# Router logits turned to token rows: transposes and an add on VectorE in place of an fp32 product

## The chip, the cores and the metric

The kernel runs on one core of one Trainium2 chip, as one launch. The metric is device time in microseconds (us). Before the change three runs took 1732.22 us in the median (1730.69 to 1737.27).

## The reference

A gated linear recurrence per head gives the token rows, and a mixture of eight experts works on them. The router weighs every expert for every token, with eight rounds of row and column normalisation (Sinkhorn) over all tokens:

```python
def _moe_ref(x, w_gate, w1, w2):          # x: 3072 tokens x 384, 8 experts, hidden size 1024
    logits = x @ w_gate
    logits = logits - logits.max()
    P = np.exp(logits)
    for _ in range(8):
        P /= P.sum(1, keepdims=True) + 1e-09
        P /= P.sum(0, keepdims=True) + 1e-09
        P *= N / E
    for e in range(E):
        h = np.maximum(x @ w1[e], 0.0)
        out += P[:, e:e + 1] * (h @ w2[e])
```

`x` is the recurrence's output: 4 sequences, 768 steps, 8 heads of 48.

## The kernel before

The work has two phases. Phase 1 runs the recurrence, and beside it the first two experts (0 and 1); phase 2 runs the other six. The change is in phase 1.

**Blocks.** The 3072 tokens are cut into 12 blocks of 256 (`SUB`), each of two chunks of 128. For block i VectorE and ScalarE prepare the gates and run a scan over them (`elem`, `chain`, `scan`): line 517 to 525 normalise (`x`, `y`, `z`), `cmul` (lines 429 to 434) is the scan's complex product, lines 535 to 546 build scaled keys (`kh`) and queries (`z` times `q`). DMAs lay keys and queries out by head (`ks` on SyncE's queue, `qs` on GpSimd's, line 569). Then `mix(i)` on TensorE transposes keys (`ktp`, line 590), makes scores (`sp`, 607), state updates (`U`, 600) and outputs (`y`, 624); VectorE masks the scores (610), carries the state (665 to 676), and splits the output into a high part `xh` and a rest `xl` (681).

**Experts.** While block i+1 is prepared and mixed, TensorE multiplies block i with experts 0 and 1 in 16 steps: `ph` (line 252, nine matmuls of 256 columns), ScalarE's `hh` and `hf` (275, 276), VectorE's rest `hl` (277), and, three steps later, `po` (213 to 215).

**Logits.** `logits(i)` is a generator that is advanced twice, after steps 1 and 3 of block i. The gate's weights are held as 16 columns, 8 high parts and 8 rests (`wgs`). Six matmuls make `lp`, 16 x 256: rows 0 to 7 from the high parts, rows 8 to 15 from the rests. ScalarE copies it to `ls`. Four steps of work later the logits are turned to token rows, 128 tokens x 8 per chunk, and put into `P`, which the Sinkhorn rounds use at the end of phase 1. `lp` and `lt` use the tag `s` of the pool `psS`, which has two buffers, as the key transposes and the scores do from block 1 on. So the buffers go round in the order in which TensorE's program asks for them: `lp`, `lt`, `ktp`, `sp`, and so on; what asks for `lt`'s buffer next is the scores.

**Order.** TensorE's order in phase 1 is written out by hand (`manual_schedule`). VectorE, ScalarE and SyncE are ordered in phase 1 by a scheduler from its own estimate of times, except for blocks 0 to 2, where lists of dependences fix part of it. Each engine works strictly along its order: what stands behind a waiting instruction waits too.

Of the kernel before, what the change touches and what calls it, by code (L numbers as in the profile page):

```python
# [6 lines left out]
F32 = mybir.dt.float32  # L7
F32R = mybir.dt.float32r
U8 = mybir.dt.uint8
AF = mybir.ActivationFunctionType  # L10
ALU = mybir.AluOpType
AX = mybir.AxisListType
# [4 lines left out]
E, F = 8, 1024  # L17
NF = F // 128
CH = 128
SUB = 256  # L20
# [56 lines left out]
class Net:  # L77
# [9 lines left out]
    def build(self):  # L87
        tc, nc = self.tc, self.nc
        DR = bass.MemoryType.DRAM
        PS = bass.MemoryType.PSUM  # L90
        with ExitStack() as ctx:
            dram = ctx.enter_context(tc.tile_pool(name="dram", bufs=1, space=DR))
            cst = ctx.enter_context(tc.tile_pool(name="cst", bufs=1))
            self.wp = ctx.enter_context(tc.tile_pool(name="wp", bufs=RING))

            self.ones = cst.tile([128, 128], F32, name="ones")
            nc.vector.memset(self.ones, 1.0)
            warm = cst.tile([128, 1], F32, name="warm")
            nc.scalar.activation(warm, self.ones[:, 0:1], AF.Abs_reciprocal_sqrt)
            self.ident = cst.tile([128, 128], F32, name="ident")  # L100
            nc.sync.dma_start(self.ident, self.idn)
            self.nident = cst.tile([128, 128], F32R, name="nident")
            self.mask = cst.tile([128, 4, CH], U8, name="mask")
            tri = cst.tile([128, CH], F32, name="tri")
            nc.sync.dma_start(tri, self.msk)
            for j in range(4):
                nc.gpsimd.tensor_copy(self.mask[:, j, :], tri)
            self.bm05 = cst.tile([128, 1], F32, name="bm05")
            nc.vector.memset(self.bm05, -0.5)
            self.wgs = cst.tile([128, NCT, 2 * E], F32R, name="wgs")  # L110
            self.two = cst.tile([2 * E, E], F32, name="two")
            nc.vector.tensor_tensor(self.two, self.ident[:2 * E, :E], self.ident[:2 * E, E:2 * E], ALU.add)
            wgr = cst.tile([128, NCT, E], F32, name="wgr")
            nc.sync.dma_start(wgr, self.wg)
            self.wgr = wgr
            self.P = cst.tile([128, self.ntt, E], F32, name="P")

            ns = self.N // SUB
            self.fl = cst.tile([128, ns * (NCT * NCH + 2) + 2 * NHALF], F32, name="fl")
            self.ok = cst.tile([128, 9], F32, name="ok")  # L120
            self.oki = cst.tile([1, 1], mybir.dt.int32, name="oki")
            self.wt = {}
            self.x_d = [dram.tile([128, NS, 2, NCT, 2, CH], F32, name=f"x_d{u}") for u in range(self.N // UN)]
            self.ye_d = [[dram.tile([128, C], F32, name=f"ye_d{u}_{i}") for i in range(self.ntt)] for u in range(2)]
            self.wd = [dram.tile([128, 4, 2 * 6 * 128], F32, name=f"wd{t}") for t in range(NT)]
            self.xf = [dram.tile([len(FORMS), 128, 2, TH], F32, name=f"xf{u}") for u in range(self.N // UN)]
            self.od = [dram.tile([128, C], F32, name=f"od{k}") for k in range(2 * NS)]

            with ExitStack() as c2, tc.manual_schedule(engines={mybir.EngineType.PE}):
                with ExitStack() as c1:  # L130
                    with ExitStack() as ca:
                        self.phase1(c1, ca)
                    self.phase2a(c2)
                with tc.manual_schedule(engines={mybir.EngineType.DVE, mybir.EngineType.Activation, mybir.EngineType.SP}):
                    self.phase2b(c2)
            flag = nc.values_load(self.oki[0:1, 0:1], min_val=0, max_val=1)
            with tc.If(flag < 1):
                with ExitStack() as c3:
                    self.general(c3)
# [557 lines left out]
    def logits(self, i):  # L697
        nc = self.nc
        xh, xl = self.xs[i]
        lp = self.psS.tile([2 * E, SUB], F32, tag="s", name=f"lp{i}")  # L700
        terms = [(ct, x) for ct in range(NCT) for x in (xh, xl)]
        if i == self.N // SUB - 1:
            terms.sort(key=lambda t: t[1] is xl)
        for q, (ct, x) in enumerate(terms):
            nc.tensor.matmul(lp, self.wgs[:, ct, :], x[:, ct, :], start=q == 0, stop=q == len(terms) - 1)
        ls = self.xp.tile([2 * E, SUB], F32, tag="ls", name=f"ls{i}", bufs=1)
        nc.scalar.activation(ls, lp, AF.Copy)
        yield
        lt = self.psS.tile([128, SUB // 128, E], F32, tag="s", name=f"lt{i}")
        for k in range(SUB // 128):  # L710
            nc.tensor.matmul(lt[:, k, :], ls[:, k * 128:k * 128 + 128], self.two, start=True, stop=True)
        n = SUB // 128
        nc.scalar.activation(self.P[:, i * n:(i + 1) * n, :], lt, AF.Copy)
        yield

    def check(self, sp, lg):
# [760 lines left out]
```

## Time and profile before

| what | value |
|---|---|
| median of three runs | 1732.22 us |
| profiled execution: span, first to last instruction | 1730.8 us |
| TensorE busy | 1707.6 us, 99% |
| VectorE busy | 1264.9 us, 73% |
| ScalarE busy | 731.4 us, 42% |
| TensorE's granted clock, mean | 0.999 |
| phase 1 | until about 586 us |

The page gives the span of the profiled execution and no other time for it. It was taken by the hardware profiler in one execution; the timed runs are other executions. "PE" in the rows is TensorE, "PEld" its weight load, "DVE" VectorE, "ACT" ScalarE, "POOL" GpSimd, "SP" SyncE. An fp32 matmul appears as several rows where the hardware takes it in passes. The share of an engine is a mean over stages: it says nothing on a stage that has another limit.

### The profile page before, as it was taken

What the parts mean: (1) busy time and instruction counts of PE and PEld (TensorE: products, weight loads), DVE (VectorE), ACT (ScalarE), POOL (GpSimd) and SP (SyncE); (2) the same over time, 40 slices, a digit from 0 to 9 for tenths busy, and PEclk for the clock granted to TensorE, in tenths of its full rate; (3) what the DMA queues carried; (4) which work ended last, traced back from release to release, by engine and by line L of the source; (5) the groups of instructions that cost most, each with busy time, mean ns of one, the idle gap of its engine ahead of it and who ended that gap; (6) DMA issues with size and microseconds to landing.
All of it is one profiled execution on the core that took longest, in us unless ns stands there. A gap on an engine that the chain in (4) does not pass through costs nothing.

```text
span 1730.8 us, 31183 instructions
## 1 busy us (share of the span) xinstructions
PE 1707.6 (99%) x11808; PEld 1677.0 (97%) x11808; DVE 1264.9 (73%) x2651; ACT 731.4 (42%) x1649; POOL 195.2 (11%) x368
## 2 busy tenths in 40 slices
PE   7999999999999999999999999999999999999998
PEld 5899999999999999999999999999999999999998
DVE  7888999899887888777755566656566655565654
ACT  8544555454543545554533333333433333433231
POOL 4211012110111323333200000000000000000000
PEclk9999999999999999999999999999999999999999
DMA  7534344543458867576567566567666556656560
GB/s 229 138 107 148 110 124 126 153 104 107 121 141 270 310 275 288 212 295 245 219 228 274 205 233 230 208 219 256 224 215 240 200 183 238 236 193 241 188 227 35
DMA packets 160829, 346.01 MB, mean 200 GB/s; under 512 B 15264, under 2 KB 101536, under 8 KB 160672
## 3 DMA queue, kind: packets, MB, share of 16 engines
q1 hardware_dynamic: 155264, 334.03, 55.5%
q0 software_dynamic: 4608, 9.52, 2.3%
q8 instruction: 95, 1.56, 0.4%
q14 instruction: 62, 0.51, 0.1%
q10 hardware_dynamic: 800, 0.39, 0.1%
HBM read 232.53 MB, written 98.70 MB: 191 GB/s over the span
## 4 chain that ended last, share of the span: by engine, by line
PE 91%; DVE 5%; DMA 2%; ACT 1%; issue 0%; SPq 0%; ACTq 0%; DVEq 0%
PE po L1089 12%; PE po L1090 12%; PE po L1088 12%; PE ph L252 10%; PE X L1144 4%; PE X L1145 4%; PE X L1146 4%; PE po L213 4%; PE po L214 3%; PE po L215 3%; PE Y L1144 3%; PE Y L1145 3%; PE Y L1146 3%; PE sp L607 2%; PE y L624 2%; PE U L600 2%
## 5 line engine op out<-in xcount | busy, mean ns | idle before, releaser
L1090 PE MATMUL po<-wd,hl 128*128 128x384 f32 x768 | 257.0, 335 | 0.0
L1089 PE MATMUL po<-wd,hh 128*128 128x384 f32 x768 | 256.6, 334 | 0.0
L1088 PE MATMUL po<-wd,hh 128*128 128x384 f32 x768 | 256.5, 334 | 0.0
L252 PE MATMUL ph<-xh,w 128*128 128x256 f32 x1152 | 225.9, 281 | 0.9 <-ACT xh L680 0.6
L252 PEld LDWEIGHTS ph<-xh,w 128*128 128x128 f32 x1152 | 185.4, 189 | 1.6 <-ACT xh L680 0.9
L252 PE MATMUL ph<-xl,w 128*128 128x256 f32 x576 | 154.5, 282 | 0.3 <-DVE xl L681 0.3
L1090 PEld LDWEIGHTS po<-wd,hl 128*128 128x128 f32 x768 | 144.2, 188 | 0.8 <-DVE hl L1166 0.2
L1088 PEld LDWEIGHTS po<-wd,hh 128*128 128x128 f32 x768 | 144.2, 188 | 0.0
L1089 PEld LDWEIGHTS po<-wd,hh 128*128 128x128 f32 x768 | 144.2, 188 | 0.0
L275 ACT ACTIVATE hh<-ph 128x256 fp32r<-128x256 f32 x160 | 61.3, 383 | 194.0 <-PE ph L252 193.4
L213 PE MATMUL po<-w,hh 128*128 128x384 f32 x384 | 138.6, 361 | 0.0
L215 PE MATMUL po<-w,hl 128*128 128x384 f32 x384 | 129.2, 336 | 0.6 <-DVE hl L277 0.6
L214 PE MATMUL po<-w,hh 128*128 128x384 f32 x384 | 129.0, 336 | 0.0
L1090 PE MATMUL po<-wc,hl 128*128 128x384 f32 x384 | 128.3, 334 | 0.0
L1089 PE MATMUL po<-wc,hh 128*128 128x384 f32 x384 | 128.3, 334 | 0.0
L1088 PE MATMUL po<-wc,hh 128*128 128x384 f32 x384 | 128.3, 334 | 0.0
L569 POOL DMA_DIRECT2D qs<-z x144 | 75.9, 535 | 424.2 <-DVE z L546 155.0
L252 PEld LDWEIGHTS ph<-xl,w 128*128 128x128 f32 x576 | 105.8, 189 | 0.5 <-DVE xl L681 0.5
L1165 ACT ACTIVATE hh<-X 128x384 fp32r<-128x384 f32 x64 | 31.5, 492 | 176.1 <-PE X L1146 176.1
L1071 DVE SCALAR_TENSOR_TENSOR oa<-po,P,oa 128x384 f32<-128x384 f32 x120 | 73.0, 614 | 20.6 <-PE po L1090 20.5
L277 DVE TENSOR_TENSOR hl<-hf,hh 128x256 fp32r<-128x256 f32 x160 | 68.6, 430 | 11.4 <-ACT hf L276 9.6
L213 PEld LDWEIGHTS po<-w,hh 128*128 128x128 f32 x384 | 72.6, 189 | 4.0 <-issue 3.4
(1826 smaller groups left out, 4396.1 us busy)
## 6 DMA issues: line engine op xcount, KB each, us to landing
wd<-wd SPq DMA_DIRECT2D x58, 768.0 KB, 5.8
wa<-wd SPq DMA_DIRECT2D x42, 768.0 KB, 4.3
wb<-wd SPq DMA_DIRECT2D x42, 768.0 KB, 5.6
wc<-wd SPq DMA_DIRECT2D x42, 768.0 KB, 4.5
xP<-xf SPq DMA_DIRECT2D x60, 384.0 KB, 4.3
raw<-in_w_dram SPq DMA_DIRECT2D x12, 1152.0 KB, 8.9
wd<-wc SPq DMA_DIRECT2D x16, 768.0 KB, 4.2
wd<-wa SPq DMA_DIRECT2D x16, 768.0 KB, 4.2
```

The costliest lines, as they stand in the source:

```text
L213: nc.tensor.matmul(po[k], hh[:, s], w2h, start=f == 0, stop=False)
L214: nc.tensor.matmul(po[k], hh[:, s], w2l, start=False, stop=False)
L215: nc.tensor.matmul(po[k], hl[:, s], w2h, start=False, stop=f == NF - 1)
L252: nc.tensor.matmul(ph, w[:, k, ct * 128:ct * 128 + 128], x[:, ct, :], start=q == 0, stop=q == len(terms) - 1)
L569: dma = eng.dma_start(dst[q:q + D - 2:NCT, :, :w], src[:, a, ct * NCH + c, :w])
L1071: V.scalar_tensor_tensor(oa[u, k], p, self.P[:, tt, e:e + 1], oa[u, k], ALU.mult, ALU.add)
L1088: nc.tensor.matmul(po[k], hh[:, s], w2[0], start=c == 1, stop=False)
L1089: nc.tensor.matmul(po[k], hh[:, s], w2[1], start=False, stop=False)
L1090: nc.tensor.matmul(po[k], hl[:, s], w2[0], start=False, stop=c == NF)
L1144: nc.tensor.matmul(ps, w[:, 0, k], x[:, 0], start=start, stop=False, skip_group_check=True)
L1145: nc.tensor.matmul(ps, w[:, 0, k], x[:, 1], start=False, stop=False, skip_group_check=True)
L1146: nc.tensor.matmul(ps, w[:, 1, k], x[:, 0], start=False, stop=True, skip_group_check=True)
```

## The change

The constant `two` (two 8 x 8 identities on top of each other) goes. Today one fp32 product per chunk, `ls` (16 x 128) as the stationary operand and `two` (16 x 8) as the moving one, turns the 16 rows to token rows and adds high part and rest; ScalarE copies the 128 x 2 x 8 result into `P`. Now a plain transpose per chunk, with a 16 x 16 identity, turns them to 128 x 16, and one VectorE reduction per block adds the halves from PSUM into `P`.

```diff
-            self.two = cst.tile([2 * E, E], F32, name="two")
-            nc.vector.tensor_tensor(self.two, self.ident[:2 * E, :E], self.ident[:2 * E, E:2 * E], ALU.add)
...
-        lt = self.psS.tile([128, SUB // 128, E], F32, tag="s", name=f"lt{i}")
-        for k in range(SUB // 128):
-            nc.tensor.matmul(lt[:, k, :], ls[:, k * 128:k * 128 + 128], self.two, start=True, stop=True)
         n = SUB // 128
-        nc.scalar.activation(self.P[:, i * n:(i + 1) * n, :], lt, AF.Copy)
+        lt = self.psS.tile([128, n, 2 * E], F32, tag="s", name=f"lt{i}")
+        for k in range(n):
+            nc.tensor.transpose(lt[:, k, :], ls[:, k * 128:k * 128 + 128], self.ident[:2 * E, :2 * E])
+        nc.vector.tensor_reduce(self.P[:, i * n:(i + 1) * n, :], lt.rearrange("p k (m e) -> p k e m", e=E), AX.X, ALU.add)
```

TensorE's order stays the same but for the two instructions of each block. The scheduler gives VectorE, ScalarE and SyncE another order in phase 1: VectorE's differs at many places, mostly by a residual `hl` that moves a few rows against a step of the recurrence. Line numbers of the changed kernel are 2 lower from line 112 on (711 is then the reduction).

On VectorE, block 0: the recurrence of block 1 is under way (`cm_a`, `cm_b` and `z` are the scan's products). Before:

```order
L432 TENSOR_TENSOR cm_a<-z_770 128x6x21 x2
L432 TENSOR_TENSOR cm_b<-z_770 128x6x21 x2
L433 TENSOR_TENSOR z_770<-cm_a,cm_b 128x6x7x3
L434 TENSOR_TENSOR z_770<-cm_a,cm_b 128x6x7x3
L432 TENSOR_TENSOR cm_a<-z_770 128x6x62 x2
```

The same place on VectorE now, with `lt` the transposed logits of block 0:

```order
L430 TENSOR_TENSOR cm_a<-z_768 128x6x21 x2
L430 TENSOR_TENSOR cm_b<-z_768 128x6x21 x2
L431 TENSOR_TENSOR z_768<-cm_a,cm_b 128x6x7x3
L432 TENSOR_TENSOR z_768<-cm_a,cm_b 128x6x7x3
L711 TENSOR_REDUCE P<-lt_990 128x16
L430 TENSOR_TENSOR cm_a<-z_768 128x6x62 x2
```

The reduction stands between two steps of the recurrence, and nothing else moved here.

On VectorE, block 5: the end of the recurrence of block 6 (`kh`, and `z` with `qk`), the start of block 7's (`x`, `y`, `z` with `x`), and residuals `hl` of the experts (`hl_4_7` is the last step of block 4, `hl_5_0` to `hl_5_3` are the first steps of block 5). Before:

```order
L545 TENSOR_TENSOR kh_4188<-x_4186,z_4088 128x1536
L521 SCALAR_TENSOR_TENSOR y_4758<-x_4757,y_4758 128x768
L681 TENSOR_TENSOR xl_3771<-y_1_3950,xh_3770 128x3x128
L546 TENSOR_TENSOR z_4088<-z_4088,qk_4089 128x12x128
L523 TENSOR_SCALAR x_4757<-y_4758 128x768
L277 TENSOR_TENSOR hl_4_7_4083<-hf_4_7_4084,hh_4_7_4082 128x256
L524 SCALAR_TENSOR_TENSOR x_4757<-zz_4759,x_4757 128x768
L277 TENSOR_TENSOR hl_5_0_4223<-hf_5_0_4224,hh_5_0_4222 128x256
L525 TENSOR_TENSOR z_4750<-z_4750,x_4757 128x12x128
L277 TENSOR_TENSOR hl_5_1_4238<-hf_5_1_4239,hh_5_1_4237 128x256
```

The same place on VectorE now:

```order
L275 TENSOR_TENSOR hl_4_7_4081<-hf_4_7_4082,hh_4_7_4080 128x256
L543 TENSOR_TENSOR kh_4186<-x_4184,z_4086 128x1536
L519 SCALAR_TENSOR_TENSOR y_4756<-x_4755,y_4756 128x768
L275 TENSOR_TENSOR hl_5_0_4221<-hf_5_0_4222,hh_5_0_4220 128x256
L544 TENSOR_TENSOR z_4086<-z_4086,qk_4087 128x12x128
L275 TENSOR_TENSOR hl_5_1_4236<-hf_5_1_4237,hh_5_1_4235 128x256
L521 TENSOR_SCALAR x_4755<-y_4756 128x768
L275 TENSOR_TENSOR hl_5_2_4273<-hf_5_2_4274,hh_5_2_4272 128x256
L522 SCALAR_TENSOR_TENSOR x_4755<-zz_4757,x_4755 128x768
L711 TENSOR_REDUCE P<-lt_4302 128x16
L523 TENSOR_TENSOR z_4748<-z_4748,x_4755 128x12x128
```

The residuals moved ahead of the steps of the recurrence: `hl_5_0` now stands before block 6's `z` with `qk`, and `hl_5_2` and the reduction before block 7's first `z`.

On VectorE, block 6: the scan of block 8. Before:

```order
L277 TENSOR_TENSOR hl_6_3_4961<-hf_6_3_4962,hh_6_3_4960 128x256
L429 TENSOR_TENSOR cm_a<-z_5430 128x12x32
L429 TENSOR_TENSOR cm_b<-z_5430 128x12x32
L433 TENSOR_TENSOR z_5430<-cm_a,cm_b 128x6x32
L434 TENSOR_TENSOR z_5430<-cm_a,cm_b 128x6x32
```

The same place on VectorE now:

```order
L427 TENSOR_TENSOR cm_a<-z_5428 128x12x32
L275 TENSOR_TENSOR hl_6_2_4935<-hf_6_2_4936,hh_6_2_4934 128x256
L427 TENSOR_TENSOR cm_b<-z_5428 128x12x32
L711 TENSOR_REDUCE P<-lt_4964 128x16
L431 TENSOR_TENSOR z_5428<-cm_a,cm_b 128x6x32
L432 TENSOR_TENSOR z_5428<-cm_a,cm_b 128x6x32
L275 TENSOR_TENSOR hl_6_3_4959<-hf_6_3_4960,hh_6_3_4958 128x256
```

The reduction stands behind `cm_b` of the last scan product of 32 columns, and the buffer of `lt`, which ScalarE's copy used to give back, is given back here.

## Rows read from the trace of the kernel before

**Rows 1.** The page's busy line: us, share of the span, instructions.
```profile
PE 1707.6 (99%) x11808; PEld 1677.0 (97%) x11808; DVE 1264.9 (73%) x2651; ACT 731.4 (42%) x1649; POOL 195.2 (11%) x368
```

**Rows 2.** TensorE's waits: who for whom, us in total, times, longest.
```profile
PE ktp L590 <- DMA ks<-kh: 1.1, 1, 1.1
```

**Rows 3.** Windows: busy us of each engine in a stretch of blocks 4 and 5.
```profile
255.00:300.00 45.00, 45.00 (x433) 44.14 (x431) 43.67 (x98) 22.15 (x55) 7.12 (x14) 1.00 0.46 125
```

**Rows 4.** The tile lt: duration ns min/median/max, first and last start.
```profile
L711 PE MATMUL lt<-two,ls x48: 251/251/272, 64.2 to 586.3; 16*128 16x8 f32 x48
L713 ACT ACTIVATE P<-lt x12: 182/190/191, 64.9 to 586.6; 128x16 f32<-128x16 f32 x12
```

**Rows 5.** Line 590, the key transposes, in the same columns.
```profile
L590 PE MATMUL ktp<-ident,ks x160: 257/259/316, 42.9 to 550.9; 112*128 112x112 f32 x160
```

**Rows 6.** Timeline of TensorE at block 5's logits: start us, us, what.
```profile
304.63 0.28 PE L252 MATMUL ph<-xh,w 128*128 128x256 f32 x1
304.84 0.61 PE L711 MATMUL lt<-two,ls 16*128 16x8 f32 x4
305.37 0.44 PE L213 MATMUL po<-w,hh 128*128 128x384 f32 x1
305.65 0.33 PE L214 MATMUL po<-w,hh 128*128 128x384 f32 x1
305.82 0.34 PE L215 MATMUL po<-w,hl 128*128 128x384 f32 x1
```

**Rows 7.** Timeline of TensorE at key transposes of block 6, then of block 3.
```profile
307.49 0.28 PE L252 MATMUL ph<-xh,w 128*128 128x256 f32 x1
307.61 0.55 PE L590 MATMUL ktp<-ident,ks 112*128 112x112 f32 x4
307.99 1.07 PE L607 MATMUL sp<-qs,ks 112*128 112x128 f32 x8
...
191.94 0.99 PE L590 MATMUL ktp<-ident,ks 112*128 112x112 f32 x8
192.70 0.42 PE L213 MATMUL po<-w,hh 128*128 128x384 f32 x1
192.95 0.33 PE L214 MATMUL po<-w,hh 128*128 128x384 f32 x1
```

**Rows 8.** Timeline of VectorE: two reductions.
```profile
580.37 0.17 DVE L725 TENSOR_REDUCE ok<-chk 128x1 f32<-128x12 f32 x1
588.90 0.27 DVE L744 TENSOR_REDUCE m<-mp 1x1 f32<-1x128 f32 x1
```

**Rows 9.** Timeline of VectorE and ScalarE at block 0's logits.
```profile
64.04 0.28 DVE L434 TENSOR_TENSOR z<-cm_a,cm_b 128x126 f32<-128x126 f32 x1
64.24 1.00 DVE L432 TENSOR_TENSOR cm_a<-z 128x372 f32<-128x372 f32 x2
64.85 0.19 ACT L713 ACTIVATE P<-lt 128x16 f32<-128x16 f32 x1
```

**Rows 10.** Timeline of VectorE and ScalarE at the first steps of block 5.
```profile
296.73 1.75 DVE L546 TENSOR_TENSOR z<-z,qk 128x1536 f32<-128x1536 f32 x1
298.91 0.38 ACT L276 ACTIVATE hf<-ph 128x256 f32<-128x256 f32 x1
300.40 1.75 DVE L525 TENSOR_TENSOR z<-z,x 128x1536 f32<-128x1536 f32 x1
```

**Rows 11.** Timeline of GpSimd at block 6's queries; DMA issues with median us to landing.
```profile
299.13 6.24 POOL L569 DMA_DIRECT2D qs<-z  x12 [33.48 <-ACT hh L275]
...
qs<-z POOLq DMA_DIRECT2D x144, 64.5 KB, 3.9
```

**Rows 12.** Timeline of VectorE and TensorE at block 6's logits and block 7's scores.
```profile
353.95 0.55 DVE L429 TENSOR_TENSOR cm_b<-z 128x384 f32<-128x384 f32 x1
...
355.50 0.73 PE L607 MATMUL sp<-qs,ks 112*128 112x128 f32 x5
```

**Rows 13.** VectorE's waits from 305 to 354.5 us.
```profile
DVE hl L277 <- ACT hf L276: 1.7, 3, 0.8
```

## The prediction, made before the changed kernel had run

> **What bounds the kernel now.** I read the busy line of the page first, then TensorE's waits, then the windows of single blocks, and only then the rows of the lines that change. The busy line [rows 1] puts TensorE at 99% of the span, VectorE at 73%, ScalarE at 42%. The reader should see that only TensorE's own time, or a new wait of TensorE, can move the end. TensorE's waits are few: behind the head, in which the weights come in, the longest single one is 1.1 us for the key tile of block 1 [rows 2], a DMA that VectorE's recurrence for that block feeds. The average share of VectorE hides its stages, so I read a stretch in which blocks 4 and 5 are worked on: in 45.00 us TensorE is busy 45.00 and VectorE 43.67 [rows 3]. There VectorE is 97% busy. It is not waited for, but it has little left to give, and the change puts work on it.
>
> **TensorE's part.** Today each block of 256 tokens issues two fp32 products; the trace has 48 passes for these 24, so two passes each, and 12 ScalarE copies of 0.19 us behind them [rows 4]. A transpose of fp32 data already stands in the kernel: 160 of them in the program (20 chunks of 8) and 160 passes in the trace [rows 5], one pass each. So a block goes from four passes to two. What a pass costs is read at block 5 [rows 6]: the four take 0.61 us and the last of them some 0.25, so they start (0.61 - 0.25) / 3 = 0.12 us apart. Two fewer are 0.24 us per block. Over 12 blocks that is 2.9 us.
>
> This has two ends. From the last matmul before the group (304.63) to the second after it (305.65) it is 1.02 us, where neighbours without the group would need 0.12 [rows 7] and 0.17 (305.65 to 305.82); so a group costs 0.73 today, and only half of that is passes. The rest is entry (0.21 instead of 0.12) and exit. Key transposes, which use 112 rows of the array, enter after 0.12, run 0.095 apart ((307.99 - 307.61) / 4) and are left after 0.25 more [rows 7]: two would fit into 0.12 + 0.19 + 0.25 = 0.56, a saving of 0.46 per block, 5.5 us in all. That is the good end. The bad end is nothing saved, if these narrow transposes take two passes each. I take 0.24, since the new transposes keep the 16-row operand of the products, the nearest row, and I see nothing in the change that touches entry and exit.
>
> The Trainium skill, "TensorEngine Tiling (Array Packing)", Key Properties, says that a change of tiling mode drains TensorE. If 16 rows count as another mode than 128, the drain stays with the transposes and the sum is 0.24 per block; if only the fp32 product caused it, it is 0.46. The late entry of the 16-row group against the 112-row one [rows 6, 7] agrees with the rule, but the trace has no 16-row transpose.
>
> **VectorE's part.** The sum of the two halves was free in the product; now a reduction of 32 values per partition, read from PSUM, does it. The trace has reductions of 12 values in 0.17 us and of 128 values from PSUM in 0.27 [rows 8]. I take 0.20; both ends stay in the range. Twelve of them are 2.4 us on VectorE, and ScalarE loses 12 x 0.19 = 2.3, which nobody was waiting for. The one small addition of two identities at the start goes too; VectorE was waiting for ScalarE before and after it, so it is worth nothing.
>
> What counts more than the 0.20 is where the reduction stands, since everything behind it on VectorE waits with it. Three places decide.
>
> Block 0. The reduction stands inside the recurrence of block 1, behind a step that ends at 64.04 + 0.28 = 64.32; the next recurrence step ran at 64.24 [rows 9]. The copy on ScalarE began at 64.85, when the products were done. With two passes fewer that is 64.6; the reduction ends at 64.8 and the recurrence goes on 0.55 us later than now. This is the chain that the 1.1 us wait hangs on, so that wait grows by 0.55, and block 0's own 0.24 is lost in it. TensorE's gain is then 11 x 0.24 = 2.6 us.
>
> Block 5. VectorE's order around it is another one: the last chain step of block 6 (z times q) now stands behind the residual of expert 0's first step of block 5, and the next chain, block 7's, behind the reduction. That residual can start when ScalarE's copy ends, 298.91 + 0.38 = 299.29, and takes 0.42; so the z step runs from about 299.75 and not from 296.73, 3.0 us later [rows 10]. Its 12 query DMAs go out over 6.24 us from 299.13 on and land 3.9 us after issue, so the sixth, with which the first chunk is complete, lands at 299.13 + 3.12 + 3.9 = 306.2, against scores that start at 307.99 [rows 7, 11]. A margin of 1.8 against 3.0: a wait of 1.2, of which I take 1.0, since both landing times are medians. The normalisation step of block 7 that ran at 300.40 cannot start before the reduction: the products end at 304.84 + 0.61 = 305.45, the transposes 0.24 earlier, the reduction at 305.4 at best. That is a chain some 5 us later [rows 6, 10].
>
> Block 6. The transposed logits sit in one of two PSUM buffers that the scores of the next block take over. ScalarE emptied it at once; now the scores wait for the reduction. It stands behind a step that runs from 353.95 to 354.50 in the old trace, and the scores start at 355.50 [rows 12]: without delay the reduction ends at 354.7 and nothing waits. But of block 7's 5 us, 1.0 is taken off by the wait above (TensorE slips too), and VectorE's idle time for hidden units, the part that can be made up, is 1.7 us between 305 and 354.5 [rows 13]. Some 2.0 us remain, so the reduction ends near 356.7 and TensorE waits 1.2. In the following blocks the same margin is used against a smaller lag; I put 0.2 us for them together.
>
> Waits: 0.55 + 1.0 + 1.2 + 0.2 = 2.95 us. With -2.6 that is +0.35 us on the profiled span of 1730.8. The page gives no other time for this execution; the span lies 1.4 us under the median of the timed runs, 1732.22, so I add the difference to the median: 1732.6 us.
>
> **Rivals.**
> - The gain is kept. VectorE catches up before anyone needs it and only block 0's 0.55 stays: 1732.2 - 2.6 + 0.55 = 1730.2. For it: later blocks are worked with far less VectorE pressure, and none of TensorE's waits in the trace is for a score mask. Against it: 43.67 of 45.00.
> - The transposes enter and leave like the key transposes: 11 x 0.46 = 5.1 saved, 0.55 lost, if nothing waits: 1727.7. For it: the same instruction in rows 7; against it: 16 rows.
> - The change doesn't do what it says: each narrow transpose takes two passes, nothing is saved and the waits stay: 1732.2 + 2.95 = 1735.2. Against it: rows 5.
> - Slower: VectorE's lag at block 5 isn't made up. The place is the PSUM buffer that the scores take over. If all 5 us arrive at block 6 and each of blocks 7 to 10 then pays 1.2 again, it is 0.55 + 1.0 + 5 + 4 x 1.2 = 11.4, less 2.6: 1741.0. It decides from the point where the chain falls behind more than 1 us per block (355.50 - 354.50). For it: 1.7 us of idle time against 5 of lag. Against it: once TensorE has waited, VectorE has that much more room.
>
> **How the numbers follow.** Chances: forecast 0.50, gain kept 0.22, quick transposes 0.08, two passes 0.08, slower 0.12. The forecast's own range is 1729 to 1737 (reductions of 0.17 to 0.27, waits of 0 to 6). The whole range of 1727 to 1739 takes in the first four and leaves the slow rival out. A change of 0.5% or 8.7 us is about what a measurement of this kernel can tell from no change. Faster by more than that needs 1723.5, beyond even the quick transposes with no wait: 0.02. Slower needs 1740.9, where the slow rival's middle is: 0.07 with a little for what I don't see. Within: 0.91.
>
> **What the profile of the changed kernel would show.** Right: 24 passes of the transposes instead of 48; some 0.8 us from the matmul before them to the second after them; 12 reductions near 0.20 us; TensorE's wait for the key tile of block 1 at 1.5 to 1.8 us; new waits of the scores for the reduction in block 6; ScalarE's 12 copies gone. The forecast is wrong if TensorE shows no new wait between 300 and 410 us, if the group takes 0.56 us, or if the scores of several blocks wait over 1 us each.

## The result and the profile after: 9.6 us slower

The changed kernel took 1741.82 us (median of five runs, 1741.45 to 1742.33) against 1732.22 (1730.69 to 1737.27): a ratio of 1.0053, with a 95% interval of 1.0042 to 1.0064. The profiled spans are 1740.6 and 1730.8 us, 9.8 apart. That is outside the predicted range of 1727 to 1739, and just over the 0.5% that the text called measurable.

The first two things to read in the new profile are the busy line of the page and the tile `lt`.

```profile
PE 1714.3 (98%) x11784; PEld 1681.9 (97%) x11784; DVE 1267.4 (73%) x2662; ACT 730.1 (42%) x1637; POOL 194.4 (11%) x368
```
```profile
L710 PE MATMUL lt<-ident,ls x24: 207/220/230, 64.2 to 589.8; 16*128 16x16 f32 x24
L711 DVE TENSOR_REDUCE P<-lt x12: 178/188/192, 64.5 to 590.2; 128x16 f32<-128x32 f32 x12
```

TensorE runs 24 instructions fewer than in [rows 1], yet is busy 6.7 us longer. The passes have halved against [rows 4], and the reduction costs 0.19 us. So what was changed did what it should. TensorE's timeline at block 5's logits, which answers to [rows 6], shows what it is worth.

```profile
304.38 0.28 PE L250 MATMUL ph<-xh,w 128*128 128x256 f32 x1
304.59 0.29 PE L710 MATMUL lt<-ident,ls 16*128 16x16 f32 x2
304.81 0.44 PE L211 MATMUL po<-w,hh 128*128 128x384 f32 x1
305.09 0.34 PE L212 MATMUL po<-w,hh 128*128 128x384 f32 x1
```

From the last matmul before the group to the second after it are 305.09 - 304.38 = 0.71 us instead of 1.02: 0.31 saved per block, 3.7 over twelve. The entry still takes 0.21 us, as before, and not 0.12.

To see where the time went I laid the two traces over one another, matmul by matmul (11,760 each, the logits' turning left out), and took each one's start in the new trace less its start in the old: the shift. A shift that grows is time lost. It goes in four stretches:

| stretch of the old trace | shift at its end | change |
|---|---|---|
| start to 306 us | -0.6 | -0.6 |
| 306 to 329 us | +5.0 | +5.5 |
| 329 to 630 us (start of phase 2) | +3.5 | -1.5 |
| 630 to 1724 us | +9.3 | +5.8 |

The last 0.5 us lie outside these matmuls, at the ends of the span. So there are two losses of nearly one size, in different phases, and they don't look alike.

**First loss: block 6's keys come late.** TensorE's waits from 295 to 340 us, and its timeline there, where [rows 7] had no gap:

```profile
PE ktp L588 <- DMA ks<-kh: 2.8, 1, 2.8
PE po L211 <- ACT yst L219: 0.6, 1, 0.6
```
```profile
306.91 0.28 PE L250 MATMUL ph<-xh,w 128*128 128x256 f32 x1
310.01 0.89 PE L588 MATMUL ktp<-ident,ks 112*128 112x112 f32 x4 [2.82 <-DMA ks<-kh]
310.69 1.94 PE L605 MATMUL sp<-qs,ks 112*128 112x128 f32 x8
312.28 0.67 PE L211 MATMUL po<-w,hh 128*128 128x384 f32 x1
312.75 0.52 PE L212 MATMUL po<-w,hh 128*128 128x384 f32 x1
```

The shift steps up by 3.0 us at 310.01. Behind the gap the matmuls are longer: 0.52 us for a row that takes 0.34 at 305.09. The windows of the same stretch show why (the number after the engines' busy times is the granted clock, as a share of full speed):

```profile
308.00:312.00 4.00, 1.99 (x11) 2.02 (x11) 3.90 (x10) 0.54 (x1) 1.26 (x3) 0.76 1.16 209
312.00:316.00 4.00, 4.00 (x29) 4.00 (x29) 3.17 (x13) 0.66 (x2) 0.00 (x0) 0.81 0.96 306
316.00:320.00 4.00, 4.00 (x44) 3.67 (x43) 3.79 (x19) 1.95 (x7) 0.00 (x0) 1.00 0.88 252
```

Means of 0.76 and 0.81 lie between the two levels, 1.2 and 2.4 GHz. After the idle 2.8 us a part of the work ran at the lower level; that is 1.7 of the 5.5 us (5.5 less the step of 3.0 and one of 0.8 at 334 us). From 316 on it is 1.00 again. So a wait of 2.8 us on the busiest engine cost some 4.7.

Why the keys are late is read backwards. SyncE's queue issues them from 300.11 on, 4.6 us later than before; 0.6 of that is the queue's own, which is busy with `xf<-x_d` until 300.02:

```profile
297.50 2.52 SPq L825 DMA_DIRECT2D xf<-x_d  x4
300.11 2.51 SPq L567 DMA_DIRECT2D ks<-kh  x4
302.72 1.01 SPq L220 DMA_DIRECT2D ye_d<-yst  x2
303.78 2.39 SPq L567 DMA_DIRECT2D ks<-kh  x2
```

The same queue in the kernel before:

```profile
295.50 1.87 SPq L569 DMA_DIRECT2D ks<-kh  x3
297.47 0.53 SPq L693 DMA_DIRECT2D x_d<-xl  x1
298.05 3.79 SPq L569 DMA_DIRECT2D ks<-kh  x6
```

The keys can be issued when VectorE has built `kh`, which starts 4.0 us later. Before, then now:

```profile
293.72 1.75 DVE L545 TENSOR_TENSOR kh<-x,z 128x1536 f32<-128x1536 f32 x1
...
297.70 1.75 DVE L543 TENSOR_TENSOR kh<-x,z 128x1536 f32<-128x1536 f32 x1
```

And `kh` is late because the recurrence of block 6 already was. VectorE's timeline, now:

```profile
278.62 0.42 DVE L275 TENSOR_TENSOR hl<-hf,hh 128x256 fp32r<-128x256 f32 x1
278.96 0.54 DVE L663 TENSOR_TENSOR tm<-st,U 112x384 f32<-112x384 f32 x1
...
279.82 0.55 DVE L670 TENSOR_TENSOR sa<-tm,rr 112x384 f32<-112x384 f32 x1
280.38 0.55 DVE L672 TENSOR_TENSOR sb<-tm,qs 48x384 f32<-48x384 f32 x1
280.95 0.55 DVE L673 TENSOR_TENSOR sb<-tm,rn 48x384 f32<-48x384 f32 x1
281.53 1.00 DVE L430 TENSOR_TENSOR cm_a<-z 128x372 f32<-128x372 f32 x2
```

And before:

```profile
277.90 0.28 DVE L434 TENSOR_TENSOR z<-cm_a,cm_b 128x126 f32<-128x126 f32 x1
278.10 0.99 DVE L432 TENSOR_TENSOR cm_a<-z 128x372 f32<-128x372 f32 x2
...
281.17 0.55 DVE L665 TENSOR_TENSOR tm<-st,U 112x384 f32<-112x384 f32 x1
...
283.07 0.55 DVE L672 TENSOR_TENSOR sa<-tm,rr 112x384 f32<-112x384 f32 x1
```

The state update (`tm`, `sa`, `sb`) used to stand among and behind these steps of the recurrence and now stands ahead of them: the step of 372 elements starts at 281.53 and not at 278.10. Its four rows make 2.2 us of these 3.4; the rest is a residual `hl` (0.3) and a delay from further ahead. So the rows that cost here are not residuals, which the section on the change names as most of what moved, and no reduction stands here. The delay lasts until `kh`. On the way VectorE even waits 1.9 us for ScalarE; in the kernel before it has no wait from 270 to 305 us:

```profile
292.21 0.96 DVE L515 SCALAR_TENSOR_TENSOR x<-sq 128x768 f32<-128x768 f32 x1 [1.87 <-ACT sq L510]
```

The chain to `kh` goes through ScalarE there (squares and roots), so the work that VectorE had done early doesn't bring the chain forward again. In a VectorE that is 97% busy [rows 3], the scheduler's other order is enough.

**Second loss: phase 2's second products run slower.** TensorE is busy 100 of 100 us there in both traces, the clock is 1.00, and the order is the same. The page's costliest group of the changed kernel, and the same instruction before (busy us, mean ns):

```profile
L1087 PE MATMUL po<-wd,hh 128*128 128x384 f32 x768 | 260.5, 339 | 0.0
```
```profile
L1089 PE MATMUL po<-wd,hh 128*128 128x384 f32 x768 | 256.6, 334 | 0.0
```

The pitch, the time from one start to the next (of those under 250 ns apart), tells more than the duration. For this product of `hh` and the weights' low part it went from 173.2 to 178.4 ns (768 of them), and for its twin with `wc` from 173.2 to 177.5 (384); for the product before it, of `hh` and the high part, from 173.7 to 174.7 (1152), and for the first products of the input forms (line 1142, which make the hidden units) from 173.9 to 172.6 (936). 0.768 x 5.2 + 0.384 x 4.3 + 1.152 x 1.0 - 0.936 x 1.3 = 5.6 of the drift's 5.8 us.

What differs there is not in the instructions. With the tile `two` went 32 bytes per partition of the SBUF pool in which the constants lie. Buffers are handed out from two ends of SBUF. Those after `two` from its end (in phase 2 the experts' weights, hidden units, copies and scratch) lie 32 bytes lower; those from the other end (input forms, staging, raw weights) stay. No row of the diff names these buffers, and no order of instructions shows that they moved.

### The profile page after: what moved, and what is told of

It reads as the page before. It is cut to its first block, busy times and chain, and to the rows that moved or that the text cites. A ratio compares the mean times of both kernels' runs of the same rounds, so it can differ in the third digit from the quotient of the medians.

```text
span 1740.6 us, 31116 instructions
## 1 busy us (share of the span) xinstructions
PE 1714.3 (98%) x11784; PEld 1681.9 (97%) x11784; DVE 1267.4 (73%) x2662; ACT 730.1 (42%) x1637; POOL 194.4 (11%) x368
## 4 chain that ended last, share of the span: by engine, by line
PE 91%; DVE 4%; DMA 2%; ACT 1%; issue 1%; SPq 0%; DVEq 0%; ACTq 0%
PE po L1087 12%; PE po L1086 12%; PE po L1088 11%; PE ph L250 9%; PE X L1142 4%; PE X L1143 4%; PE X L1144 4%; PE po L211 3%; PE po L213 3%; PE po L212 3%; PE Y L1142 3%; PE Y L1143 3%; PE Y L1144 3%; PE sp L605 2%; PE y L622 2%; PE V L1142 1%
## 5 line engine op out<-in xcount | busy, mean ns | idle before, releaser
L1087 PE MATMUL po<-wd,hh 128*128 128x384 f32 x768 | 260.5, 339 | 0.0
L1086 PE MATMUL po<-wd,hh 128*128 128x384 f32 x768 | 258.5, 337 | 0.0
```

The costliest lines, as they stand in the source:

```text
L1086: nc.tensor.matmul(po[k], hh[:, s], w2[0], start=c == 1, stop=False)
L1087: nc.tensor.matmul(po[k], hh[:, s], w2[1], start=False, stop=False)
```

## The experiments

**Theory A**: the slower phase 2 comes from the 32 bytes. **Theory C**: the loss of phase 1 comes from the order that the scheduler chose. **Theory D**, the rival: from the reductions as work on VectorE. Each run had five rounds or more beside the kernel before, which took 1731.9 to 1732.2 us. "Drift" is what the shift grows by from 630 us to the end. A pad is an unused tile. In each kernel line numbers move by the lines put in.

**The changed kernel with the 32 bytes put back** (`e1_after_pad32`); the order of every engine is that of the changed kernel.

```diff
+            pad = cst.tile([128, 8], F32, name="pad")
             wgr = cst.tile([128, NCT, E], F32, name="wgr")
```

> The changed kernel with an unused tile of 32 bytes per partition where the constant of the two identities stood. The order on every engine is that of the changed kernel; only the SBUF addresses of what is allocated behind that tile go up by 32 bytes, to where they were before the change. Theory A (the steady loss of phase 2, 3.5 us of lag at 622 us against 9.2 at 1703, comes from the addresses): 1741.8 - 5.8 = 1736.0 us, and the matmuls of hh with the low part of the second weights are 173 ns apart again and not 178. Theory B (it comes from something that TensorE carries over from its wait at 307 us, or from the transposes): 1741.8 us, 178 ns.

Measured: 1737.22 us, 1.0033 (1.0021 to 1.0045), 4.6 less than without the pad. The shift is +4.2 at 630 us and +4.2 at 1724; the product of `hh` and the low part takes 173.5 ns again, on the page 256.6 us (the pad's line makes it line 1088):

```profile
L1088 PE MATMUL po<-wd,hh 128*128 128x384 f32 x768 | 256.6, 334 | 0.0
```

The key wait stays (3.5 us at the place that had 2.8). Theory A holds, and the two losses are separate.

**The kernel before with 32 bytes more** (`e2_before_pad32`), so that the same buffers stand 32 bytes higher; order as before.

```diff
+            pad = cst.tile([128, 8], F32, name="pad")
             wgr = cst.tile([128, NCT, E], F32, name="wgr")
```

> The kernel before with an unused tile of 32 bytes more per partition behind the constant of the two identities; nothing else. Theory A (addresses): the weights' ring sits 32 bytes off its old place, so phase 2 is slower by about 5.8 us: 1738 us, with 178 ns from matmul to matmul in hh times low weights. Theory B: 1732.2 us, 173 ns.

Measured: 1742.15 us, 1.0058 (1.0044 to 1.0072). The shift is +0.5 at 630 us and +12.3 at the end. This time the product of `hh` with the weights' *high* part is slow, 173.7 to 179.0 ns (768) and 178.0 (384), while its neighbour stays at 173.5. Of the 12 us, about 5 are waits of TensorE for VectorE's sums (line 1158) between 640 and 790 us, which the expectation (1738 us) had not foreseen; the profiled execution is the slowest of the five, 1744.88:

```profile
PE Z L1145 <- DVE 21_3_9419 L1158: 1.6, 1, 1.6
PE Z L1145 <- DVE 21_9_10566 L1158: 1.5, 1, 1.5
PE Z L1145 <- DVE 21_7_10191 L1158: 1.0, 1, 1.0
```

An unused tile alone, with no other edit, makes a kernel 0.6% slower. That is as much as the whole change did.

**The kernel before with 64 bytes more** (`e3_before_pad64`).

```diff
+            pad = cst.tile([128, 16], F32, name="pad")
             wgr = cst.tile([128, NCT, E], F32, name="wgr")
```

> The kernel before with an unused tile of 64 bytes per partition behind the constant; order unchanged. Theory A1 (what counts is the address modulo 64 bytes): 1732 us, all three second-layer matmuls 173 to 174 ns apart. Theory A2 (any shift of the left-hand buffers against what does not move costs): slower by 5 us or more.

Measured: 1737.8 us, 1.0034 (1.0022 to 1.0046), with a drift of 5.8 us. The low-part product is at 180.6 ns, the high-part one at 175.4, but the first products of the input forms fell from 173.9 to 169.3 (936 of them, 4.3 us back). So it isn't a step with a period of 64 bytes; each distance tried has its own pattern.

**The second loss, taken apart.** Three runs put 32 bytes into the changed kernel at one place each, the order untouched. `e8_pad_hidden`: ahead of phase 2's hidden units (they, the copies and the scratch move up, the weights do not). `e9_pad_copies`: behind the hidden units (only copies and scratch move). `e10_pad_right`: at the other end, so that input forms, staging and raw weights move *down* as all else has.

```diff
+        pad = c2.enter_context(tc.tile_pool(name="pad", bufs=1)).tile([128, 8], F32, name="pad")    # e8
         self.hp = c2.enter_context(tc.tile_pool(name="hp2", bufs=2))
+        pad = c2.enter_context(tc.tile_pool(name="pad", bufs=1)).tile([128, 8], F32, name="pad")    # e9
...
+        pad = c2.enter_context(tc.tile_pool(name="pad", bufs=1, side="right")).tile([128, 8], F32, name="pad")    # e10
         xa = c2.enter_context(tc.tile_pool(name="xa", bufs=1, side="right"))
```

> The changed kernel with 32 unused bytes put in only ahead of phase 2's hidden units, so that hidden units, copies and phase 2's scratch stand 32 bytes higher in SBUF (where they stood in the kernel before) while the experts' weights stay 32 bytes lower. The order of every engine is that of the changed kernel. Theory H (the place of the hidden units decides the pitch of the second products): the 1152 products with the low second weights go back from 178 to 173.4 ns, the drift over phase 2 goes, 1736 to 1737.3 us. Rival W (the place of the weights decides): pitch 178, drift 5.8 us, 1741.8 us. If only their distance decides, neither: a third pitch, anywhere from 1731 to 1748 us.

> The changed kernel with the 32 unused bytes behind the hidden units instead: only ScalarE's copies of phase 2 and its scratch stand higher. Theories H and W both: nothing of the second products' operands has moved, pitch 178, 1741.8 us (1741 to 1743). If the engines that write and read the copies and the scratch beside the matmuls decide the pitch: 173.4 ns and 1736 to 1737.3 us.

> The changed kernel with the 32 unused bytes on the other side of SBUF, so that phase 2's input forms, their staging and the raw weights stand 32 bytes lower, as all else already does: the distances between all of phase 2's buffers are those of the kernel before, only the absolute place is 32 bytes lower. If the distance between buffers decides: 173.4 ns, 1736 to 1737.3 us. If the place of the hidden units or of the weights by itself decides: 178 ns, 1741.8 us. The products of the input forms (line 1142 to 1144) may change their pitch of 173 either way by 4 ns in a third of their 2800, 4 us.

| run | us | ratio (interval) | `hh` x high, x low part, ns (768 with `wd`) | drift from 630 us |
|---|---|---|---|---|
| changed kernel | 1741.82 | 1.0053 (1.0042 to 1.0064) | 174.8, 178.4 | +5.8 |
| hidden units up | 1739.76 | 1.0042 (1.0028 to 1.0056) | 172.4, 175.2 | +3.6 |
| copies up | 1743.53 | 1.0069 (1.0055 to 1.0083) | 174.8, 178.4 | +5.8 |
| other end down | 1737.49 | 1.0028 (1.0017 to 1.0038) | 173.7, 173.3 | -0.1 |

The last run settles it: all of phase 2's buffers stand 32 bytes lower than in the kernel before, the distances between phase 2's buffers are the old ones, and every pitch is the old one to 0.1 ns. The page agrees, in the words of its group for the low part:

```profile
L1088 PE MATMUL po<-wd,hh 128*128 128x384 f32 x768 | 256.5, 334 | 0.0
```

The distance between the buffers of the two ends decides, not their place. Copies and scratch have no part in these pitches. The medians of the last two runs lie a little above what was expected (by 0.5 and 0.2 us); their drift doesn't, so that excess is phase 1's. Moving the hidden units back takes off 2.2 of the 5.8 us of drift, and makes a third pattern, as that expectation allowed. Which two accesses meet is not settled: the slow product reads only weights and hidden units, which kept their distance in the changed kernel, so an access to the other end beside it (results, input forms, transfers) is likely the partner. That is inferred; no run tells which.

**The addition on GpSimd** (`e4_pool_add`): transposes, pad, and no reduction on VectorE.

```diff
-        nc.vector.tensor_reduce(self.P[:, i * n:(i + 1) * n, :], lt.rearrange("p k (m e) -> p k e m", e=E), AX.X, ALU.add)
+        lc = self.xp.tile([128, n, 2 * E], F32, tag="lc", name=f"lc{i}", bufs=1)
+        nc.scalar.activation(lc, lt, AF.Copy)
+        nc.gpsimd.tensor_tensor(self.P[:, i * n:(i + 1) * n, :], lc[:, :, :E], lc[:, :, E:], ALU.add)
```

> The transposes of the change with the old addresses (pad of 32 bytes), but no reduction on VectorE: ScalarE copies the transposed logits out of PSUM, GpSimd adds the halves. VectorE's order around block 5 is still the scheduler's new one, with the residuals ahead of the recurrence. Theory C (the new order makes the keys of block 6 late): the wait of 2.8 us for the key tile and TensorE's low clock behind it stay, 1735 to 1737 us. Theory D (the reduction in VectorE's queue makes them late): the wait goes, 1736 - 4.5 = 1731.5 us.

Measured: 1742.02 us, 1.006 (1.0046 to 1.0073), above both ranges. With no reduction on VectorE the key wait of block 6 is there as in the changed kernel, since the scheduler chose nearly that kernel's order (`kh` at 298.27). So the reductions are not needed for the wait, and theory D falls for it. What lies above the range comes later: another 3.1 us are lost where the Sinkhorn rounds start: the product `mp` needs the last rows of `P`, and GpSimd's last addition stood behind its sums of raw weights and ran at 594.72 us; `mp` started at 595.42. The row on `mp` names no releaser, which "issue" stands for:

```profile
PE ktp L589 <- DMA ks<-kh: 4.2, 2, 2.8
PE mp L744 <- issue: 3.1, 1, 3.1
```

**The product kept, its copy moved to VectorE** (`e6_product_dve_copy`), which adds 12 instructions of 0.17 us there.

```diff
-        nc.scalar.activation(self.P[:, i * n:(i + 1) * n, :], lt, AF.Copy)
+        nc.vector.tensor_copy(self.P[:, i * n:(i + 1) * n, :], lt)
```

> The kernel before with one edit: VectorE, not ScalarE, copies the product's result from PSUM into the routing table. No transposes, no moved addresses; the scheduler's order around block 5 stays as before, with the 12 copies put in. Theory C: VectorE's part alone costs next to nothing, 1732 to 1733 us. Theory D: it alone costs some us, 1735 or more, with a wait for keys near 307 us.

Measured: 1732.32 us, 1.0005 (0.9996 to 1.0014), and the shift is +0.04 at the end. Here the scheduler kept nearly the old order: with the two traces compared row by row (by name and shape), 13 of VectorE's 2651 rows stand elsewhere, against 134 in the changed kernel. Twelve more short instructions on VectorE cost nothing by themselves.

**Three residuals pinned behind the chain** (`e5_pinned`, pad included): what the prediction had blamed, undone alone.

```diff
+            if i == 6:
+                post, norm = self.dve[6, 0], self.dve[7, "n0"]
+                for a, b in ((norm[3], self.rest[4, 15]), (norm[4], self.rest[5, 0]), (norm[5], self.rest[5, 1])):
+                    tc.add_manual_dep(b.ins, a.ins.name, edge, reason="chain ahead of the rests")
```

> The change with the old addresses (pad of 32 bytes) and with the reduction on VectorE, but three dependences keep the residuals of three expert steps (the last of block 4, the first two of block 5) behind the steps of the recurrence that stood ahead of them in the kernel before. Theory C (order): the wait for block 6's keys goes, and with it the low clock, 4.5 us: 1731.5 us. Theory D (reduction): the wait stays, 1736 us.

Measured: 1736.2 us, 1.0025 (1.0016 to 1.0034); missed. The scheduler rearranged even more around the pins (187 rows by the same comparison), and TensorE waited for other things, most of all for residuals. The first row here is such a wait, the second shows the keys:

```profile
PE po L214 <- DVE hl L276: 3.0, 3, 1.7
...
298.24 1.75 DVE L549 TENSOR_TENSOR kh<-x,z 128x1536 f32<-128x1536 f32 x1
```

The key wait at 307 us is gone, but not because the keys came earlier: `kh` started at 298.24, half a microsecond later than in the changed kernel, with the state update ahead of the recurrence as there. TensorE, held 1.7 us by a residual at 303 us, reached the keys only at 309.89. So the residuals that the prediction had blamed did not make the keys late, and pinning one place moves the loss; it doesn't restore the order.

**The whole change and the pad, in the order of before** (`e7_order_of_before`). VectorE's, ScalarE's and SyncE's instructions of phase 1 are chained in the old kernel's order by dependences without a semaphore; only the reductions find their own place.

```diff
+            for a, b in zip(order, order[1:]):
+                tc.add_manual_dep(b.ins, a.ins.name, edge, reason="the order of the kernel before")
```

> The change (transposes, reduction on VectorE) with the old addresses (pad of 32 bytes), and with VectorE, ScalarE and SyncE held in phase 1 to the very order that they have in the kernel before; only the 12 reductions are put in and the 12 copies and the sum of two identities are left out. Theory C (what phase 1 lost came from the scheduler's new order): 12 x 0.31 = 3.7 us are gained by the transposes, VectorE's 12 x 0.2 cost little, 1728.5 to 1730.5 us, and no wait for keys at 307 us. Theory D (the reduction in VectorE's queue costs it): still 1734 us or more.

Measured: 1730.93 us, 0.9996 (0.9987 to 1.0005), span 1729.2: 6.3 us under the run with the pad alone, and no key wait in block 6. Theory C holds, though the time is 0.4 us above its range, and the interval against the kernel before includes 1. Which of the three engines' orders counts was not tried apart. The shift falls by 0.32 with each block's logits, to -2.1 by block 9, and ends at -1.3. The rest goes to two small waits at 537 and 582 us (+0.5, +0.8), whose cause no run shows, and to block 0. There VectorE holds the recurrence for the reduction, as the prediction said (the step of 372 began at 64.24 before; 0.39 us of its 0.79 come from the kernel's head; recorded instructions all carry line 87 here):

```profile
64.93 0.19 DVE L745 TENSOR_REDUCE P<-lt 128x16 f32<-128x32 f32 x1 [0.23 <-PE lt L744]
65.03 0.99 DVE L87 TENSOR_TENSOR cm_a<-z 128x372 f32<-128x372 f32 x2
```

TensorE's waits from 50 to 100 us in this run (line 301 is the product that takes the hidden units `hh`; before it waited 0.4):

```profile
PE ktp L622 <- DMA ks<-kh: 1.2, 1, 1.2
PE ph L301 <- ACT hh L87: 1.1, 1, 1.1
```

**Block 0's reduction behind the recurrence** (`e11_reduction_late`), else as the last run.

```diff
+        tc.add_manual_dep(self.red0.ins, self.nc.made["vector"][88].ins.name, edge, reason="behind the recurrence of block 1")
```

> The changed kernel in the order of the kernel before, with the pad, and with the reduction of block 0 moved behind the last step of block 1's recurrence (behind the first state product, in an idle gap of VectorE of 0.45 us); all else as in the run with the order of before. Theory (the reduction delays the recurrence of block 1 by 0.4 us and TensorE pays 0.7 us at 71 us in a wait for ScalarE's hidden units): that wait goes from 1.1 back to 0.4 and the time from 1730.9 to 1730.2 us, ratio 0.9990 against the kernel before. Rival (the delay of 0.4 us at the start came from the head, not from the reduction): the wait stays above 0.8 and the time at 1730.9.

Measured: 1729.89 us, 0.9989 (0.998 to 0.9998): by the medians 2.3 us faster than the kernel before. Both of the waits above shrink:

```profile
PE ktp L622 <- DMA ks<-kh: 0.7, 1, 0.7
PE ph L301 <- ACT hh L87: 0.7, 1, 0.7
```

The wait for `hh` didn't go all the way back to 0.4, since TensorE itself arrives 0.2 us earlier (`hh` starts at 70.64, at 70.55 in the kernel before). The reduction ran at 69.23 us, in the gap. The shift at the end is -3.0: of the 3.8 us that the transposes save (12 x 0.32), most is kept once the two side effects are gone. Against the last run that is 1.7 more, of which 0.9 are these two waits; the rest is an earlier start (0.3) and the wait at 537 us, which isn't there this time. This beats the kernel before by 0.1%, just clear of the interval.

## Why the prediction was wrong, point by point

- **TensorE's part: mechanism right, size a little low.** Two passes per block instead of four, as said. The saving is 0.31, not 0.24, inside the bounds of 0 and 0.46, because the transposes follow each other faster: 0.07 us apart (0.29 - 0.22) where the products were 0.12. The 0.71 us from the matmul before to the second after answer to "some 0.8 us". Entry and exit stayed: 0.21 us in, and 0.28 from the first matmul behind to the second. The quick entry of the 112-row transposes was not to be had. The Trainium skill, "TensorEngine Tiling (Array Packing)", Key Properties, says that a change of tiling mode drains TensorE; the 0.21 of the 16-row transposes agrees with it, though no run shows that 16 rows count as another mode.
- **The reduction: right.** 0.19 against 0.20, and twelve short instructions more on VectorE cost nothing by themselves, shown by the run with the copy on VectorE (ratio 1.0005). Of the reductions only block 0's has a price that a run traces to it.
- **Block 0: right in mechanism, at another wait.** The recurrence went on 0.38 us later (64.62 for 64.24), less than 0.55 because the transposes were done at 64.5. The price fell on the wait for hidden units at 71 us, which grew from 0.4 to 1.1, not on the key wait, which was to grow from 1.1 to between 1.5 and 1.8 and shrank to 0.4 in the changed kernel. With the reduction put behind the recurrence, the shift at the end goes from -1.3 to -3.0 and the median from 1730.9 to 1729.9 (the two intervals overlap). The step and the waits of the changed kernel, then the wait of the kernel before:

```profile
64.62 0.99 DVE L430 TENSOR_TENSOR cm_a<-z 128x372 f32<-128x372 f32 x2
...
PE ph L267 <- ACT hh L264: 1.1, 1, 1.1
PE ktp L588 <- DMA ks<-kh: 0.4, 1, 0.4
...
PE ph L269 <- ACT hh L266: 0.4, 1, 0.4
```

- **Block 5: the failed step of phase 1.** The step of z times q that was to run "3.0 us later", with 1.0 us of wait for queries, took the chain of block 6 as on time up to there, and priced only the one residual in the quoted rows. The chain was already 3.4 us late at 281.53 (`tm`, `sa` and `sb` had moved ahead, some 15 us before the place that the prediction quoted). So the keys failed first, on SyncE, and the queries did not: TensorE lost 3.0 us at the key tile and waited for no query. And a wait was counted as its length; with the lower clock behind it the loss was 4.7.
- **Block 6 and the later blocks: wrong.** The 1.4 us of waits put there did not come: nothing of TensorE waited for the reduction. The slow rival gave 1741.0, next to the measured 1741.8, by a PSUM buffer that never became late; its number was met by chance.
- **Phase 2: the omitted step.** The prediction took for granted that what the diff doesn't touch keeps its time. Of the addition of two identities it says that "it is worth nothing": it looked at the instruction and not at the 32 bytes that the tile held. That term, put at nothing, was 5.8 us of drift, and 4.6 in the median once the bytes were put back.
- **The gain kept (1730.2):** it is what the change is worth with both side effects taken away: 1730.9 and 1729.9.

## What to carry to other kernels

Removing a tile moves every buffer handed out after it, and an engine that is 100% busy can lose half a per cent by that alone: before judging an edit, run it with the freed bytes put back. Where a scheduler sets the order and an engine is 97% busy, an edit is two edits, itself and a new order; compare the order from the first row that differs, not only around the new instruction, or pin the old one to see what the edit itself is worth. An average busy share doesn't price a wait of TensorE: add what the clock takes behind it.

## What the hardware showed that I had not expected

- The pitch of 128x384 products, with TensorE without a gap and at full clock, changes when the distance between SBUF buffers changes by 32 or 64 bytes: 173 to 174 ns in the kernel before, up to 180.6 and down to 169.3 with 64 bytes more. A row that got slower and one that got faster stood in the same kernel. No distance tried was better in sum than the old one. The Trainium skill, "SBUF — State Buffer", Who interferes with whom, says that only the port pair that VectorE and GpSimd share causes contention. If the slow pitches are contention, they differ from that, and the measurement decides; what TensorE meets there is open.
- After 2.8 us without work the granted clock fell to means of 0.76 and 0.81 from 308 to 312 and from 312 to 316 us, at a cost of about 1.7 us beside the wait.
- Two 16-row fp32 transposes take 0.22 us each, with 0.07 between their starts, and cost about 0.42 as a group (0.71 less the 0.12 and 0.17 of neighbours), of which the passes are the smaller part.
